# One more chunk in the seven-product form: the second layer of a fused FFT filter and two-layer network on one Trainium2 core

## The chip, the cores and the metric

The kernel runs on one core of one Trainium2 chip. The metric is the device time of one execution in microseconds (us), the median over several executions of the same program; lower is better. Engines are named as the profile names them: PE is TensorE's matmul, PEld its weight load, DVE is VectorE, ACT is ScalarE, POOL is GpSimd, SP is the queue on SyncE that issues most transfers.

## The reference, cut to what matters

```python
# x: 8 x 3008 x 256, filter: 1505 x 256 complex, w_in: 256 x 2048, w_out: 2048 x 256
X = np.fft.rfft(x, axis=1)
Y = X * (filt_r + 1j * filt_i)[None]
y = np.fft.irfft(Y, n=3008, axis=1)          # 8 x 3008 x 256
h = y.reshape(24064, 256) @ w_in             # 24064 x 2048
g = np.maximum(0.01 * h, h)
out = g @ w_out                              # 24064 x 256
```

## The kernel before, in words

**Two layers by chunks.** The 24064 tokens are cut into 47 chunks of 512 (`NCHUNK`, counted from 0). `moe1` computes the first layer of a chunk: per 128 columns of `w_in` two matmuls into one half of a wide PSUM tile `ph` (L514), and after each pair of halves one ACT activation of 1024 columns into `gt_c` (L519). The second layer of chunk `ci` is spread over the time in which `moe1` works on chunk `ci + 1`; this stretch is called the slot of chunk `ci` below.

**Two forms of the second layer.** `plain(ci)` multiplies `gt_c` by `w_out`: 4 token tiles of 16 matmuls with 256 columns (L681), each tile emptied by a DVE copy (L686) and stored. `products(ci)` treats the multiplication as a 2 x 2 block product and does it with seven half-size products instead of eight: 7 x 16 matmuls of 128 columns (L589). For this DVE builds four sums of 128 x 2048 elements beforehand (`act_sums`, L555; three go into `big[0]`, one over a quarter of `gt_c`), and every product is emptied by its own addition on DVE (L617, L625, L633, L639, L642, L653) or by an ACT copy (m1, L629). The sums of the weights, `wt_sb`, are built early, at planned times 10 to 11.5. The seventh product, `last_product`, needs the last sum and is done in the slot of the next chunk; its place in the first slot of the form is filled with sixteen items that do nothing.

`W0 = 3` says from which chunk on the second layer uses `products`; chunks 0, 1 and 2 use `plain`.

**Banks.** Tiles of the second layer alternate between two PSUM banks, `out_banks`: `psp_last` (named `pf` in the profile, the third of the `pf` tiles) and `po_ps`. `product` picks its bank when the list of work is built; `plain` picks it when the work is issued, from the final count of products:

```python
po = out_banks[(done["products"] + tj) % 2].rearrange("p a t d -> p (a t d)")[:, :D]
```

**The FFT of the next batches beside it.** Between these matmuls lie the four steps of the next batch's filtering, each with one of two more banks (`pf`): `s1_group` (L259, emptied by ACT at L262), `s2_group` (two matmuls L308, emptied by DVE with products by the filter: L314, L315 and L320 for even groups of batch 1, L317 and L320 for the others), `sa_group` (L330, emptied by ACT L332) and `sb_group` (L351, emptied into `yt` at L341). For odd groups SP moves the halves of a product across partitions (L318, L319). POOL then adds both products into `y` (L323), the moving operand of L330. POOL also issues the loads of `x` (L196). Transfers through DRAM, issued by SP, turn the data between the steps: stores L264 and L334, loads L271 and L278.

**Order.** Nothing is scheduled at run time. Every step gets a planned time (`at`, with 8 units for a slot) and the program is written in the order of these times, so each engine executes its own list in that fixed order and waits on semaphores. `plan` and the queue below it place the FFT steps. The items of the second layer are spread evenly over a slot, the sums at the offsets `SUMS`.

Of the kernel before, what the change touches and what calls it, by code (L numbers as in the profile page):

```python
# [75 lines left out]
def kernel(  # L76
# [19 lines left out]
    SL = 8  # L96
    NCH = NCT // 2
    QT = 4 * N1
    W0 = 3
    GAP = 0.6  # L100
    EXG = 0
    LANDED = 2.43
# [512 lines left out]
    def last_product(ci):  # L615
        def after(po):
            add(rows(ci, 0)[:, :, 1], po, rows(ci, 1)[:, :, 2], AL.add)  # L617
            soon(AFTER[5], lambda: stores(ci, 0))
        return product(ci, lambda: sum_places(ci)[3], b22, after, 3)

    def products(ci):
        a11, a12, a21, a22 = (lambda i=i, j=j: quarter(ci, i, j) for i in range(2) for j in range(2))

        def after5(po):
            add(rows(ci, 1)[:, :, 1:3], twice(po), part[1], AL.add)  # L625
            soon(AFTER[5], lambda: stores(ci, 1))

        def m1():
            return product(ci, a11, b11, lambda po: nc.scalar.copy(t1, po))  # L629

        def m2(early=None):
            def after(po):
                add(rows(ci, 0)[:, :, 0], po, t1, AL.add)  # L633
                if early is not None:
                    soon(0.3, lambda: [store(ci, 2 + t, rows(ci, 0)[:, t, 0], 0, P) for t in range(2)])
            return product(ci, a12, b21, after)

        def m7():
            return product(ci, lambda: sum_places(ci)[1], wt[2], lambda po: add(v7, po, t1, AL.add), 1)  # L639

        def m6(of=None):
            return product(ci, lambda: sum_places(ci)[2], wt[1], lambda po: add(part[1], twice(po), part[0], AL.add), 2, of)  # L642

        if ci == NCHUNK - 1:
            free = [w[:, :CH].rearrange("p (a t d) -> p a t d", a=2, t=2)[:, 0] for w in wide + single]
            return last_product(ci - 1) + m1() + m7() + m2(ci) + m6(free[0]) + last_three(ci, free[1:])
        if ci > W0:
            items = m1() + last_product(ci - 1) + m2() + m7()
        else:
            done["products"] += 1  # L650
            items = m1() + [lambda: None] * (2 * NCH) + m2() + m7()
        items += m6()
        items += product(ci, a22, wt[3], lambda po: add(rows(ci, 1)[:, :, 0], po, u3, AL.add))  # L653
        return items + product(ci, lambda: sum_places(ci)[0], wt[0], after5, 0)

    def last_three(ci, free):

        free += [b[:, 0] for b in out_banks]
        low, high = rows(ci, 0), rows(ci, 1)

        def m4_tile(t, po):
            add(high[:, t, 0], po, u3[:, t], AL.add)
            parts = list(pieces(ci, t, high[:, t, 0:2, :].rearrange("p k d -> p (k d)")))
            parts.sort(key=lambda v: -v[1].shape[0])
            soon(0.02, lambda: (nc.sync, nc.scalar)[t].dma_start(*parts[0]))
            for v in parts[1:]:
                soon(0.6, lambda v=v: nc.sync.dma_start(*v))

        def m3_tile(t, po):
            add(low[:, t, 1], po, high[:, t, 2], AL.add)  # L670
            soon(0.02, lambda: store(ci, 2 + t, low[:, t, 1], P, P, queue=(nc.sync, nc.scalar)[t]))

        items = product(ci, lambda: sum_places(ci)[0], wt[0], lambda po: add(high[:, :, 1:3], twice(po), part[1], AL.add), 0, free[0])
        items += product(ci, lambda: quarter(ci, 1, 1), wt[3], None, of=[f[:, 0] for f in free[1:3]], each=m4_tile)
        return items + product(ci, lambda: sum_places(ci)[3], b22, None, 3, of=[f[:, 0] for f in free[3:5]], each=m3_tile)

    def plain(ci):

        def one(tj, ct):
            po = out_banks[(done["products"] + tj) % 2].rearrange("p a t d -> p (a t d)")[:, :D]  # L680
            nc.tensor.matmul(po, gts[ci][:, ct, ts(tj, P)], w_out_sb[:, ct, :],  # L681
                             start=(ct == 0), stop=(ct == NCT - 1))
            if ct < NCT - 1:
                return
            ot = outp.tile([P, D], FP32, tag="ost", padded_shape=[P, 6 * P], name=f"ost_c{ci}_t{tj}")
            nc.vector.tensor_copy(ot[:], po)  # L686
            soon(AFTER[5], lambda: store(ci, tj, ot[:]))
        return [lambda tj=tj, ct=ct: one(tj, ct) for tj in range(4) for ct in range(NCT)]
# [70 lines left out]
    for ci in range(NCHUNK + 1):  # L759
# [3 lines left out]
        if ci == 0:  # L763
            continue
        wino = W0 <= ci - 1
        items = products(ci - 1) if wino else plain(ci - 1)
# [38 lines left out]
```

## Time and profile before

| what | value |
|---|---|
| median of 3 runs | 747.57 us (746.96 to 748.95) |
| profiled execution: its own time, first to last instruction (span) | 745.2 us |
| median less that span | 2.4 us |
| granted TensorE clock | 0.999 |
| busy, share of the span | PE 99%, PEld 71%, DVE 68%, ACT 75%, POOL 22% |
| L681, plain second layer (3 chunks) | 192 matmuls |
| slot of chunk 2, 80.37 to 97.09 us | PE 16.72, DVE 8.23, ACT 12.85, POOL 9.23 busy |
| slot of chunk 3, 97.09 to 112.02 us | PE 14.77, DVE 7.08, ACT 13.58, POOL 0.00 busy |

Only the span is listed for the profiled execution, not a total of its own; the three runs beside it are separate. The matmul rows of a timeline give the start and the modelled duration up to the result; since matmuls are pipelined, what one costs is the distance from start to start. A slot is found in the timeline by its first second-layer matmul.

### The profile page before, as it was taken

The numbers are of one execution on the slowest core, as the hardware profiler recorded it, in microseconds if no ns is written. First come the engines' busy times: TensorE is split into PE (matmuls) and PEld (weight loads), VectorE is DVE, ScalarE is ACT, GpSimd is POOL, SyncE is SP. The second block draws the span as 40 slices with busy tenths as digits, with TensorE's granted clock in tenths as the row PEclk, the third lists the DMA queues.
The fourth block names the chain that finished last, engine by engine and source line by source line (L and its number), as shares of the span: only waits on it lengthen the run. The fifth ranks groups of instructions, "written<-read, shape, count | busy, mean of one in ns | idle before, by whom it ended". The sixth has DMA issues, their size and how long they took to land.

```text
span 745.2 us, 19416 instructions
## 1 busy us (share of the span) xinstructions
PE 738.0 (99%) x8017; PEld 528.9 (71%) x8017; DVE 504.6 (68%) x686; ACT 559.1 (75%) x755; POOL 166.2 (22%) x171
## 2 busy tenths in 40 slices
PE   9999999999999999999999999999999999999997
PEld 3556667677687777877778777777777777777776
DVE  5987637766776766766777667766677676465566
ACT  4776787888878787877777787787777777777762
POOL 6503412332232212121232222121212210000000
PEclk9999999999999999999999999999999999999999
DMA  9997797888876666655675656543554333111012
GB/s 207 229 224 197 191 224 216 209 195 208 216 181 147 159 186 176 169 138 163 193 178 150 159 155 175 156 139 109 144 160 119 106 103 103 60 55 55 29 46 70
DMA packets 119848, 113.64 MB, mean 152 GB/s; under 512 B 16384, under 2 KB 93056, under 8 KB 119568
## 3 DMA queue, kind: packets, MB, share of 16 engines
q1 hardware_dynamic: 104425, 94.73, 42.9%
q0 software_dynamic: 15056, 17.49, 15.8%
q8 instruction: 62, 1.02, 0.6%
q14 instruction: 26, 0.21, 0.1%
q10 hardware_dynamic: 279, 0.19, 0.1%
HBM read 57.51 MB, written 50.33 MB: 145 GB/s over the span
## 4 chain that ended last, share of the span: by engine, by line
PE 96%; DMA 1%; DVE 1%; ACT 1%; issue 0%; ACTq 0%; DVEq 0%
PE ph L514 43%; PE pf L589 18%; PE po_ps L589 18%; PE pf L259 3%; PE pf L351 3%; PE pf L308 2%; PE pf L330 2%; PE po_ps L373 1%; PE pf L681 1%; PE po_ps L681 1%; DMA dz<-big 1%; DMA big<-dz 0%; ACT yt L341 0%; PE pf L442 0%; PE ph L401 0%
## 5 line engine op out<-in xcount | busy, mean ns | idle before, releaser
L519 ACT ACTIVATE gt_c<-ph 128x1024 f16<-128x1024 f32 x376 | 385.3, 1025 | 133.5 <-PE ph L514 122.8
L514 PE MATMUL ph<-yt,w_in_sb 128*128 128x512 f16 (+7 forms) x1728 | 447.3, 351 | 0.2 <-ACT yt L341 0.2
L589 PEld LDWEIGHTS <-gt_c 128*128 128x128 f16 x2800 | 202.2, 98 | 91.1
L323 POOL TENSOR_TENSOR y_b_g<-p_b_g,p_b_g 128x512 f16<-128x512 f32 x84 | 116.4, 1388 | 414.9 <-DMA p_b_g<-p_b_g 249.9
L589 PEld LDWEIGHTS <-big 128*128 128x128 f16 x2128 | 151.2, 98 | 61.4
L514 PEld LDWEIGHTS <-w_in_sb 128*128 128x128 f16 x1728 | 137.5, 98 | 19.7 <-DVE yt L341 0.4
L317 DVE TENSOR_TENSOR p_b_g<-pf,fb_sb 128x512 f32<-128x512 f32 x78 | 53.7, 688 | 31.0 <-PE pf L308 13.8
L589 PE MATMUL po_ps<-wt_sb,gt_c 128*128 128x128 f16 x704 | 70.0, 219 | 0.0
L589 PE MATMUL pf<-wt_sb,gt_c 128*128 128x128 f16 x688 | 68.4, 219 | 0.0
L589 PE MATMUL pf<-w_out_sb,gt_c 128*128 128x128 f16 x720 | 67.9, 219 | 0.0
L589 PE MATMUL pf<-wt_sb,big 128*128 128x128 f16 x704 | 67.2, 219 | 0.0
L262 ACT CAST big<-pf 128x512 f16<-128x512 f32 x98 | 57.1, 588 | 11.9 <-PE pf L259 10.5
L589 PE MATMUL po_ps<-w_out_sb,gt_c 128*128 128x128 f16 x688 | 66.0, 219 | 0.0
L589 PE MATMUL po_ps<-wt_sb,big 128*128 128x128 f16 x688 | 65.3, 219 | 0.0
L341 ACT CAST yt<-pf 128x376 f16<-128x376 f32 x120 | 56.4, 473 | 10.9 <-PE pf L351 8.0
L555 DVE TENSOR_TENSOR big<-gt_c 128x2048 f16<-128x2048 f16 (+1 forms) x46 | 58.7, 1276 | 0.1
L555 DVE TENSOR_TENSOR gt_c<-gt_c 128x2048 f16<-128x2048 f16 x43 | 57.4, 1335 | 1.0
L320 DVE TENSOR_TENSOR p_b_g<-pf,fa_sb 128x512 f32<-128x512 f32 x84 | 57.2, 681 | 0.2
L555 DVE TENSOR_TENSOR big<-gt_c,big 128x2048 f16<-128x2048 f16 (+1 forms) x45 | 55.3, 1230 | 0.0
L555 DVE TENSOR_TENSOR big<-big,gt_c 128x2048 f16<-128x2048 f16 (+1 forms) x45 | 55.2, 1227 | 0.1
L332 ACT CAST big<-pf 128x512 f16<-128x512 f32 x84 | 49.0, 584 | 4.9 <-PE pf L330 3.0
L259 PE MATMUL pf<-x_sb,small_sb 94*128 94x512 f16 x109 | 41.6, 381 | 0.0
(97 smaller groups left out, 625.9 us busy)
## 6 DMA issues: line engine op xcount, KB each, us to landing
dz<-big SPq DMA_DIRECT2D x98, 256.0 KB
p_b_g<-p_b_g SPq DMA_DIRECT2D x156, 128.0 KB
out_dram<-ost_c_h SPq DMA_DIRECT2D x118, 128.0 KB
big<-dz SPq DMA_DIRECT2D x42, 256.0 KB
big<-dz SPq DMA_DIRECT2D x56, 192.0 KB
x_sb<-in_x_dram POOLq DMA_DIRECT2D x40, 192.0 KB, 4.4
x_sb<-in_x_dram POOLq DMA_DIRECT2D x2, 768.0 KB, 9.1
w_in_sb<-in_moe_w_in_dram POOLq DMA_DIRECT2D x1, 1024.0 KB, 13.2
```

Of the source, the lines that this page charges most:

```text
L259: nc.tensor.matmul(ps, fwd1[:N1], x_sb[:N1, ds(2 * g, 2), :], start=True, stop=True)
L262: copy(st[:, ds(2 * (g % 2), 2), :], ps)
L317: nc.vector.tensor_tensor(p2[:], ps, fb, AL.mult)
L320: nc.vector.tensor_tensor(p1[:], ps, fa, AL.mult)
L323: ("y", b, g), lambda: nc.gpsimd.tensor_tensor(y1[:], p1[:], p3[:], AL.add)))
L332: nc.scalar.copy(st2[h % 4][:, ds(2 * (g % 2), 2), :], ps)
L341: copy(yv, ps.rearrange("p c a -> p a c"))
L351: nc.tensor.matmul(ps[:, j, :], z2[h % 4][:K4, j, ts(dt, P)], i1_sb[:K4, 4 * h + j, :], start=True, stop=True)
L514: nc.tensor.matmul(ph[:, j, ds(t - ci * CH, e - t)], w_in_sb[:, dt, ts(ct, P)], yt[:, dt, ds(t % N, e - t)], start=(dt == 0), stop=(dt == ...
L519: nc.scalar.activation(gts[ci][:, ds(2 * g, 2), :], ph, AF.Lrelu)
L555: nc.vector.tensor_tensor(*(v[:, ds(c0, n)] for v in (o, i0, i1)), op)
L589: nc.tensor.matmul(of[t], a()[:, c, ts(t, P)], w[:, c, :], start=(c == 0), stop=(c == NCH - 1))
```

## The change

The constant that says from which chunk on the seven-product form is used goes from 3 to 2, so that the second layer of chunk 2 is done by `products` and no longer by `plain`:

```diff
-    W0 = 3
+    W0 = 2
```

What follows from the one constant in the issued program: in the slot of chunk 2 (after 64 matmuls L681 are gone) there are six products, with the sixteen empty items after the first; the seventh product of chunk 2 stands in the slot of chunk 3, where the empty items were. DVE gets 4 sums L555 and 6 additions there and loses 4 copies L686; ACT gets one copy L629. Of the stores, four tiles of `ost_c` spread over the slot become two groups of three stores, the first behind L625 at the end of the slot, the second behind L617 in the next slot. The number of products rises from 305 to 312, so the tiles of `plain` in chunks 0 and 1 swap their banks: the last tile of chunk 1 now lies in `po_ps`, as does the first product of chunk 2. The FFT steps keep their order.

## The prediction

> **What bounds the kernel now.** First the page's busy time and the head of its chain, then the timeline around the slot of chunk 2, then the waits.
>
> ```profile
> PE 738.0 (99%) x8017; PEld 528.9 (71%) x8017; DVE 504.6 (68%) x686; ACT 559.1 (75%) x755; POOL 166.2 (22%) x171
> ...
> PE 96%; DMA 1%; DVE 1%; ACT 1%; issue 0%; ACTq 0%; DVEq 0%
> ```
>
> PE never rests, at a granted clock of 0.999; the list of waits on PE holds six entries of 1.2 us or less. So PE work that goes away is gained in full, and any new wait of PE is lost in full, since PE is as full after it as before.
>
> Timeline of PE (start, duration, engine, line):
>
> ```profile
> 52.02 0.60 PE L681 MATMUL pf<-w_out_sb,gt_c 128*128 128x256 f16 x4
> 52.46 0.59 PE L514 MATMUL ph<-yt,w_in_sb 128*128 128x512 f16 x2
> ...
> 85.91 0.38 PE L330 MATMUL pf<-y_b_g,small_sb 128*128 128x512 f16 x1
> ...
> 92.21 0.38 PE L330 MATMUL pf<-y_b_g,small_sb 128*128 128x512 f16 x1
> ...
> 108.04 0.55 PE L589 MATMUL po_ps<-wt_sb,gt_c 128*128 128x128 f16 x7
> 108.43 0.59 PE L514 MATMUL ph<-yt,w_in_sb 128*128 128x512 f16 x2
> ```
>
> Start to start, a plain matmul costs 0.44/4 = 0.109 us, a product matmul 0.39/7 = 0.0557 us. The two L330 are marks for later: each may only start when DVE's L320 has emptied the same bank.
>
> **The gain.** 64 x 0.109 = 6.98 us go, 112 x 0.0557 = 6.24 us come: -0.74 us on PE. In place: the slot of chunk 2 loses 6.98 and gets 96 x 0.0557 = 5.35 (-1.63), the slot of chunk 3 gets 16 x 0.0557 = 0.89 more. On POOL and SP no instruction is added but two groups of stores for four.
>
> The Trainium skill, "TensorE: Matmul & The Clock Gate", section "Back-to-back issue gap", speaks against the change: streams of weight load and matmul are to settle at about 81 ns per matmul for 128 columns. The 0.0557 above disagrees; by the page the products would cost 112 x 0.081 = 9.07 us (an estimate), and PE would lose 2.1 us instead of gaining 0.74.
>
> **The DVE list in the slot.** DVE is busy 8.23 of 16.72 us there. Added are 4 L555 of 1.22 = 4.88 and additions of 0.42 + 0.42 + 0.69 + 0.42 + 0.69 = 2.64; four copies of 0.42 go. 14.1 of some 16 us is room on average, but the list is in fixed order, and each sum stands ahead of something PE waits for. DVE before:
>
> ```profile
> 80.14 0.42 DVE L686 COPY ost_c_t<-pf 128x256 f32<-128x256 f32 x1 [1.52 <-PE pf L681]
> ...
> 84.71 0.68 DVE L320 TENSOR_TENSOR p_b_g<-pf,fa_sb 128x512 f32<-128x512 f32 x1
> ...
> 91.01 0.68 DVE L320 TENSOR_TENSOR p_b_g<-pf,fa_sb 128x512 f32<-128x512 f32 x1
> ```
>
> Step by step, with 0.06 us from an end to PE's start (a guess; 0 to 0.15):
>
> 1. Bank. The last tile of chunk 1 and the first product now share `po_ps`. The copy L686 ends at 80.56, PE is there at 80.37, and starts at 80.65 by two roundings: **+0.28** (0.2 to 0.4). Before, it took the other bank and waited for nothing.
>
> 2. The empty items. Between L330 of group 4 and L308 of group 9, which use one bank, lay five L681 and a pair L514 (0.98 us); now one L589 and two L514 (0.49 us). ACT's L332 takes 0.42 from L330's start to its own (82.43 to 82.85) and 0.58: PE arrives about 0.4 early. **+0.44** (0.2 to 0.5).
>
> 3. The sums ahead of group 9. DVE: L555 80.59 to 81.81; L314, L315, L320 (0.70 + 0.71 + 0.61) to 83.83; the second L555 to 85.05; L317 0.60; L320 85.65 to 86.34, against 85.39 before. PE's L330 of group 5 stood at 85.91; by then 23 L681 (2.51) are replaced by 25 L589 (1.39), and 0.72 was lost: 85.51. It starts at 86.40: **+0.89** (0.6 to 1.1).
>
> 4. POOL. A DVE sum and POOL's L323 do not run together. Later in the run:
>
> ```profile
> 207.33 1.22 DVE L555 TENSOR_TENSOR big<-gt_c 128x2048 f16<-128x2048 f16 x1
> 208.58 2.17 DVE L555 TENSOR_TENSOR gt_c<-gt_c 128x2048 f16<-128x2048 f16 x1
> ...
> 207.40 2.27 POOL L323 TENSOR_TENSOR y_b_g<-p_b_g,p_b_g 128x512 f16<-128x512 f32 x1 [7.20 <-DVE p_b_g L320]
> ```
>
> The first L555 takes its usual 1.22, L323 lasts a microsecond over its 1.27, the next L555 a microsecond over its 1.22: they take turns. In this slot L323 now meets sums. `y` of group 8 becomes ready at 83.9 behind the second L555, runs 85.05 to 86.3; the third L555 then runs to 87.5; `y` of group 7 holds to 88.8. DVE's L314 of group 10 overwrites what that L323 reads, so it starts at 88.8 (87.62 before). Then 2.02, the fourth L555 1.22, L639 0.42: 92.5. The fifth product's bank waits for this L639, PE being there at 92.26: **+0.29** (0 to 0.6). L317 0.60 and L320 to 93.8. PE's L330 of group 7 stood at 92.21; 47 L681 (5.12) against 67 L589 (3.73) and 1.90 lost: 92.72. It waits to 93.8: **+1.10** (0.5 for no meeting with POOL, 1.4 if POOL takes two turns).
>
> The waits sum to 3.0 us.
>
> 5. Transfers. Before, PE lost 0.16 at 109.24 to the load L278 of turned data (issued 106.21, landing 2.98 later), behind the last store L334 (issued 100.69, 5.51 to land). Behind the three stores of chunk 2, held by L625 to about 99.2 and issued at 0.82 each (98.18, two in 1.65), L334 comes 1.5 later; the second group of stores puts 256 KB, 0.9 us at the 280 GB/s of that stretch, ahead of L278: 2.4 later in all. PE is 2.26 later there. So the 0.16 stays, between 0 and 0.5 if the queues drain otherwise. The `x` loads on POOL move 2.1 (92.51 to 94.6) behind L323; the next L259 that needs one stood at 100.36, and moves too; landing takes 3.6 to 7.7 us. Nothing is lost in the middle case, up to 1 in the late one.
>
> 6. The rest. ACT gets one L629 of 0.39 beside 12.85 of 16.72 busy: nothing, since its L519 waited 0.17 to 0.8 on PE here; without that cover it is 0.27 once. Swapped banks later on are the same two banks in turn: nothing. In the slot of chunk 3, L617 and a sum that starts about 1.4 us late sit on a DVE busy 7.08 of 14.93 us: nothing, and 0.4 if a bank is missed.
>
> Sum: -0.74 + 3.0 = **+2.3 us**. The profiled span goes from 745.2 to 747.5; what lies around it, 2.4 us to the median, stays: 747.57 + 2.3 = **749.9 us**.
>
> **The rivals.**
>
> *Covers hold.* The waits do not form, since DVE has 2 us of room on average and PE often runs one bank ahead: -0.74 us, 746.8. For it speaks that PE hardly waited beside the some 170 sums of later slots; against it that the list of groups 8 to 11 has no later slot's spacing and that L330 trails L320 by only 0.5 us before (85.39 to 85.91). It decides if L320 of group 9 ends before 85.5.
>
> *No meeting with POOL.* Steps 1 to 3 with 0.65 in step 4: +1.5 us, 749.1. It holds if L323 lies beside PSUM work only; the fixed order speaks against.
>
> *Late transfers.* Delayed L323 and L625 push `x` loads and L278 past PE, each once by 0.5 to 1.5: +3.3 to +5 us, 750.9 to 752.6. For it: 5.51 us for one store and 2.98 for one load on the way to PE already; against: PE comes 2.3 us later as well.
>
> *Weight loads pace the products.* If loads didn't overlap, 112 x 0.098 (mean of a weight load) = 10.98 us, +4.0 in place of -0.74, and with the waits +7. The x7 row says no. The page of the Trainium skill named above, "TensorE: Matmul & The Clock Gate", gives a milder form of this rival.
>
> **How the numbers follow.** Forecast 0.50, late transfers 0.27, no meeting 0.12, covers hold 0.08, weight loads 0.03. A measurement of this kernel tells about 0.3%, 2.24 us, from no change; the forecast lies on that bound, 0.27 of its 0.50 above. Slower by over 0.3%: 0.27 + 0.27 + 0.03 = 0.57. Within: 0.23 + 0.12 + 0.05 = 0.40. Faster: 0.03, covers that hold and a scatter of the runs as wide as before's 2 us. The range leaves out most of the covers case and the top of the late one: 747.5 to 751.8. Its low end is the sum of the low ends of the waits, 1.5, less 0.74, and another 0.8 for scatter; its high end is that of the high ends, 4.0 less 0.74, and the 1 of late transfers.
>
> **What would show it.** PE waits named to DVE of about 0.3, 0.9, 0.3 and 1.1 and one to ACT of 0.4, all between 80 and 94; PE's busy sum 0.74 lower; L323 of group 8 at 85, lasting over 2 us with its wait; slot of chunk 2 near 18.1 us long (16.72 - 1.63 + 3.0) and of chunk 3 near 15.8 (14.93 + 0.89). If PE waits for a DMA by over 0.5 us after 98, the late case is it; no wait over 0.2 in the slot makes the forecast wrong.

## The result, and the profile after

The changed kernel takes 750.75 us (median of 8 runs, 748.41 to 752.74), the kernel before beside it 747.88 (8 runs, 746.54 to 749.28). The ratio is 1.004, interval 1.0031 to 1.005: slower by 2.9 us, 2.3 to 3.7. The forecast was 749.9, slower by 2.3.

A part of every time lies outside the span. The forecast put it at 2.4 us, the difference between a median and the span of another execution, and let it stay. Run by run it is 2.1 to 2.3 us in the 57 executions of the kernel before that stand beside the experiments, and 1.8 to 1.9 in the eight of the changed kernel. So the span grew by some 0.3 us more than the time did; no run explains this difference.

The profiled execution has a span of 750.4 us against 745.2 and took 752.28 in all, 1.5 above the median of its kernel. The 5.2 us between the two spans are therefore not the effect of the change alone, and what follows goes by single places. First line 1 of the page:

```profile
PE 739.0 (98%) x8065; PEld 529.1 (71%) x8065; DVE 509.3 (68%) x692; ACT 560.1 (75%) x756; POOL 168.4 (22%) x171
```

The matmuls are 48 more (112 for 64), and PE has 1.0 us more busy time, where 0.74 less was forecast. Busy time runs to the modelled end of the last matmul ahead of each wait, and there are more waits now; the starts below are the better measure. The list of waits on PE (sum, times, longest, in us) has new entries, and the one for L278 stood at 0.2 before:

```profile
PE pf L330 <- DVE p_b_g L320: 1.5, 2, 0.9
PE pf L351 <- DMA big<-dz: 1.5, 1, 1.5
...
PE pf L330 <- POOL y_b_g L323: 0.6, 1, 0.6
...
PE pf L308 <- ACT big L332: 0.2, 1, 0.2
```

The entry for POOL is a wait at 542.17, taken up under "Left open"; the timeline of PE shows where the others are (the bracket is idle time after the modelled end of the matmul before; from start to start the loss is about 0.17 larger):

```profile
80.28 0.59 PE L514 MATMUL ph<-yt,w_in_sb 128*128 128x512 f16 x2
80.96 0.55 PE L589 MATMUL po_ps<-w_out_sb,gt_c 128*128 128x128 f16 x7
...
83.15 0.59 PE L514 MATMUL ph<-yt,w_in_sb 128*128 128x512 f16 x2
83.93 0.38 PE L308 MATMUL pf<-big,f_sb 128*128 128x256 f16 x2 [0.19 <-ACT big L332]
...
85.40 0.50 PE L589 MATMUL pf<-w_out_sb,gt_c 128*128 128x128 f16 x6
86.57 0.38 PE L330 MATMUL pf<-y_b_g,small_sb 128*128 128x512 f16 x1 [0.67 <-DVE p_b_g L320]
...
92.25 0.33 PE L589 MATMUL pf<-wt_sb,big 128*128 128x128 f16 x3
92.75 0.33 PE L589 MATMUL po_ps<-wt_sb,gt_c 128*128 128x128 f16 x3 [0.17 <-DVE big L639]
93.94 0.38 PE L330 MATMUL pf<-y_b_g,small_sb 128*128 128x512 f16 x1 [0.87 <-DVE p_b_g L320]
...
98.58 0.39 PE L589 MATMUL po_ps<-w_out_sb,gt_c 128*128 128x128 f16 x4
...
100.78 0.44 PE L589 MATMUL pf<-w_out_sb,big 128*128 128x128 f16 x5
101.36 0.38 PE L330 MATMUL pf<-y_b_g,small_sb 128*128 128x512 f16 x1
...
111.55 0.22 PE L589 MATMUL pf<-wt_sb,gt_c 128*128 128x128 f16 x1
113.27 0.35 PE L351 MATMUL pf<-i_sb,big 96*128 96x94 f16 x4 [1.50 <-DMA big<-dz]
```

The rows of the kernel before on which the last line of the table below and the shift rest:

```profile
79.94 0.59 PE L514 MATMUL ph<-yt,w_in_sb 128*128 128x512 f16 x2
...
108.86 0.22 PE L589 MATMUL po_ps<-wt_sb,gt_c 128*128 128x128 f16 x1
109.24 0.35 PE L351 MATMUL pf<-i_sb,big 96*128 96x94 f16 x4 [0.16 <-DMA big<-dz]
```

Each loss is the start of the waiting matmul less the start of the row above it and that row's matmuls at 0.0557 (L589) or 0.2165 (L514) each. The first product: 80.96 - 80.28 - 2 x 0.2165 = 0.25. By the same rule L351 lost 0.32 before and 1.66 after.

| place | forecast | measured |
|---|---|---|
| bank of the first product, 80.96 | 0.28 | 0.25 |
| L308 behind ACT's L332, 83.93 | 0.44 | 0.35 |
| L330 of group 5 behind L320 of group 9, 86.57 | 0.89 | 0.84 |
| bank of the fifth product, 92.75 | 0.29 | 0.33 |
| L330 of group 7, 93.94 | 1.10 | 1.02 |
| L330 of group 11 behind POOL, 101.36 | 0 | 0.30 |
| L351 behind L278, 113.27 | 0 (to 0.5) | 1.34 more than before |

The first five sum to 2.79 (3.0 forecast). The slot of chunk 2 goes from 80.71, when the L514 of 80.28 are through, to 98.58: 17.87 us, 18.1 forecast. The slot of chunk 3 goes on to 116.06: 17.48 us, where 15.8 was forecast. With the gain of 0.74 and the last two rows the net is 3.69; from the starts of L351, 113.27 - 109.24 = 4.03, less the 0.34 by which this slot began later (L514 at 80.28 against 79.94), it is the same. DVE and POOL beside it:

```profile
80.48 0.42 DVE L686 COPY ost_c_t<-po_ps 128x256 f32<-128x256 f32 x1 [1.52 <-PE po_ps L681]
...
84.10 1.22 DVE L555 TENSOR_TENSOR gt_c<-gt_c 128x2048 f16<-128x2048 f16 x1
...
85.83 0.68 DVE L320 TENSOR_TENSOR p_b_g<-pf,fa_sb 128x512 f32<-128x512 f32 x1
86.43 2.32 DVE L555 TENSOR_TENSOR big<-big,gt_c 128x2048 f16<-128x2048 f16 x1
...
92.28 0.41 DVE L639 TENSOR_TENSOR big<-po_ps,big 128x256 f32<-128x256 f32 x1
...
93.21 0.68 DVE L320 TENSOR_TENSOR p_b_g<-pf,fa_sb 128x512 f32<-128x512 f32 x1
```

```profile
84.33 3.33 POOL L323 TENSOR_TENSOR y_b_g<-p_b_g,p_b_g 128x512 f16<-128x512 f32 x2 [4.24 <-PE pf L308]
...
91.38 3.34 POOL L323 TENSOR_TENSOR y_b_g<-p_b_g,p_b_g 128x512 f16<-128x512 f32 x2 [3.23 <-DVE p_b_g L320]
...
99.29 2.02 POOL L323 TENSOR_TENSOR y_b_g<-p_b_g,p_b_g 128x512 f16<-128x512 f32 x1 [3.58 <-PE pf L259]
101.26 1.53 POOL L196 DMA_DIRECT2D x_sb<-in_x_dram  x3
```

DVE has no idle time from the copy L686 to the end of L642; before, it had idle time in this stretch. Where a sum meets L323, one of the two is 0.8 to 1.1 us longer: the third L555 takes 2.32 for 1.22, two L323 take 3.33 for the 2.50 that they take without sums.

### The profile page after: what moved, and what is told of

Its sections match the earlier page's. It is cut to its first block, busy times and chain, and to the rows that moved or that the text cites. A ratio compares the mean times of both kernels' runs of the same rounds, so it can differ in the third digit from the quotient of the medians.

```text
span 750.4 us, 19518 instructions
## 1 busy us (share of the span) xinstructions
PE 739.0 (98%) x8065; PEld 529.1 (71%) x8065; DVE 509.3 (68%) x692; ACT 560.1 (75%) x756; POOL 168.4 (22%) x171
## 4 chain that ended last, share of the span: by engine, by line
PE 80%; DMA 5%; POOL 1%; SPq 1%; issue 0%; DVE 0%; ACT 0%; POOLq 0%; DVEq 0%
PE ph L514 37%; PE po_ps L589 17%; PE pf L589 17%; DMA p_b_g<-p_b_g 3%; PE pf L351 2%; PE pf L259 2%; PE pf L330 2%; PE pf L308 2%; POOL y_b_g L323 1%; DMA dz<-big 1%; DMA big<-dz 0%; SPq L318 0%; PE ph L589 0%; SPq L575 0%; SPq L271 0%
## 5 line engine op out<-in xcount | busy, mean ns | idle before, releaser
L514 PE MATMUL ph<-yt,w_in_sb 128*128 128x512 f16 (+7 forms) x1728 | 447.5, 351 | 0.2 <-ACT yt L341 0.2
L589 PEld LDWEIGHTS <-gt_c 128*128 128x128 f16 x2864 | 206.8, 98 | 95.9 <-issue 2.8
L323 POOL TENSOR_TENSOR y_b_g<-p_b_g,p_b_g 128x512 f16<-128x512 f32 x84 | 118.6, 1414 | 418.9 <-DMA p_b_g<-p_b_g 249.5
L589 PEld LDWEIGHTS <-big 128*128 128x128 f16 x2176 | 154.9, 98 | 63.2
L514 PEld LDWEIGHTS <-w_in_sb 128*128 128x128 f16 x1728 | 136.9, 98 | 20.1 <-issue 1.1
L317 DVE TENSOR_TENSOR p_b_g<-pf,fb_sb 128x512 f32<-128x512 f32 x78 | 53.6, 687 | 30.4 <-PE pf L308 15.3
L589 PE MATMUL po_ps<-w_out_sb,gt_c 128*128 128x128 f16 x752 | 71.2, 219 | 0.1
L589 PE MATMUL pf<-wt_sb,gt_c 128*128 128x128 f16 x720 | 71.0, 219 | 0.0
L589 PE MATMUL po_ps<-wt_sb,gt_c 128*128 128x128 f16 x704 | 70.6, 219 | 0.2 <-DVE big L639 0.2
L589 PE MATMUL pf<-wt_sb,big 128*128 128x128 f16 x720 | 68.7, 219 | 0.0
L589 PE MATMUL po_ps<-wt_sb,big 128*128 128x128 f16 x704 | 67.2, 219 | 0.0
L589 PE MATMUL pf<-w_out_sb,gt_c 128*128 128x128 f16 x688 | 65.8, 219 | 0.0
L555 DVE TENSOR_TENSOR big<-gt_c 128x2048 f16<-128x2048 f16 (+1 forms) x47 | 59.3, 1262 | 0.1
L555 DVE TENSOR_TENSOR gt_c<-gt_c 128x2048 f16<-128x2048 f16 x44 | 58.0, 1319 | 1.0
L320 DVE TENSOR_TENSOR p_b_g<-pf,fa_sb 128x512 f32<-128x512 f32 x84 | 57.1, 680 | 0.2
L555 DVE TENSOR_TENSOR big<-big,gt_c 128x2048 f16<-128x2048 f16 (+1 forms) x46 | 56.9, 1238 | 0.1
L555 DVE TENSOR_TENSOR big<-gt_c,big 128x2048 f16<-128x2048 f16 (+1 forms) x46 | 55.8, 1214 | 0.0
L332 ACT CAST big<-pf 128x512 f16<-128x512 f32 x84 | 49.0, 584 | 6.7 <-PE pf L330 4.8
```

The source lines that it names most:

```text
L317: nc.vector.tensor_tensor(p2[:], ps, fb, AL.mult)
L320: nc.vector.tensor_tensor(p1[:], ps, fa, AL.mult)
L323: ("y", b, g), lambda: nc.gpsimd.tensor_tensor(y1[:], p1[:], p3[:], AL.add)))
L332: nc.scalar.copy(st2[h % 4][:, ds(2 * (g % 2), 2), :], ps)
L514: nc.tensor.matmul(ph[:, j, ds(t - ci * CH, e - t)], w_in_sb[:, dt, ts(ct, P)], yt[:, dt, ds(t % N, e - t)], start=(dt == 0), stop=(dt == ...
L555: nc.vector.tensor_tensor(*(v[:, ds(c0, n)] for v in (o, i0, i1)), op)
```

## The experiments

Every ratio is to the kernel before on the same chip. In the traces the *shift* is by how much later than before ACT's L629 of chunk 4 starts, less the shift that was there already when the slot of chunk 2 began; it is 3.69 for the changed kernel. "Landing" is the time from the issue of the store L334 that holds back L278 to the issue of L278. A trace is one execution. Those of e1 and e7 lie 1.5 and 2.3 us above the median of their runs, those of e6 and e4 0.9 and 2.1 below; those of the other experiments lie within 0.8. Where the work is the same, the waits in the slot of chunk 2 repeat from trace to trace; a wait for a transfer in one of these four need not be that of a median run.

### e2: without the sums

The forecast's theory puts nearly all of the loss on the four sums of chunk 2, since all that PE waits for stands behind them.

```diff
-        nc.vector.tensor_tensor(*(v[:, ds(c0, n)] for v in (o, i0, i1)), op)
+        if ci != 2:
+            nc.vector.tensor_tensor(*(v[:, ds(c0, n)] for v in (o, i0, i1)), op)
```

> W0 = 2, the four sums of chunk 2 on DVE left out (its products read what lies there). Theory: PE's waits on L320 (0.84 and 1.02 us) and on the bank of L639 (0.33) go, the waits on the bank (0.25) and on ACT (0.35) stay, so PE comes out of the slot 2.2 us earlier than in the changed kernel. L625 and L617 then come earlier too, but the load L278 waits for its own store: PE may wait there 0.5 to 2 us. Over the kernel before: 0 to +1.5 us. Rival (transfers alone make the loss): the time stays within 0.5 us of the changed kernel, +2.4 to +2.9.

Measured: 747.57, ratio 1.0002 (0.9993 to 1.0011); shift -0.47. Of the new waits of PE, one stays:

```profile
PE pf L308 <- ACT big L332: 0.2, 1, 0.2
```

The bank of the first product still costs its 0.25 by the starts (80.81 - 80.13 - 2 x 0.2165), too short for the list. L351 no longer waits (landing 5.90). With the 0.32 that L351 lost before, -0.74 + 0.25 + 0.35 - 0.32 = -0.46 is the shift. The products, the empty items, the additions and the regrouped stores are all still there and cost little; the loss needs the sums, the wait for L278 included.

### e5: the sums alone

The other way round: chunk 2 stays `plain`, and DVE gets the four sums at their places, into buffers that nobody reads then.

```diff
+    def spare_sum(step):
...
+        for step, time in enumerate(SUMS if ci == W0 else ()):
+            at(SL * ci + time, lambda step=step: spare_sum(step))
```

> W0 = 3 as before; only four sums of the operands of chunk 2 are added on DVE at the times at which the changed kernel has them, into buffers that nobody reads, and chunk 2 stays plain. PE's work is that of the kernel before. Theory (the sums on DVE, not the products, cost the time): L320 of groups 9 and 11 end near 86.4 and 93 to 94 as in the changed kernel, the third sum meets L323 and takes over 2 us, PE waits 0.3 to 0.6 on the first and 1.0 to 1.5 on the second, and again on L278: +1.5 to +3 us over the kernel before. Rival (the order of PE's new items, the empty items and the banks make the loss): within 0.5 us of the kernel before.

Measured: 751.43, ratio 1.0055 (1.0042 to 1.0068), more than expected; shift +3.7. Its waits of PE, and the fourth sum, which here meets L323 (the third does too, with 2.00):

```profile
94.55 0.38 PE L330 MATMUL pf<-y_b_g,small_sb 128*128 128x512 f16 x1 [1.63 <-DVE p_b_g L320]
...
113.16 0.35 PE L351 MATMUL pf<-i_sb,big 96*128 96x94 f16 x4 [1.74 <-DMA big<-dz]
```

```profile
91.05 2.25 DVE L563 TENSOR_TENSOR big<-gt_c,big 128x2048 f16<-128x2048 f16 x1
```

Neither product nor bank nor store was changed, and the time is lost at three of the same places: by the starts 0.31 at L330 of group 5 (too short for a bracket), 1.79 at L330 of group 7 and 1.58 more than before at L351, 3.68 together and so all of the shift. The expectation named all three, gave no size for the wait for L278, and had too little for that on group 7 (1.0 to 1.5). With e2: the sums in DVE's list cause the loss, and are enough for it.

### e1: the bank of the first product

```diff
-            po = out_banks[(done["products"] + tj) % 2]...
+            po = out_banks[(done["products"] + tj + 1) % 2]...
```

> W0 = 2, but the plain tiles of chunks 0 and 1 get the banks that they had with W0 = 3, so the last tile of chunk 1 and the first product of chunk 2 no longer share po_ps. Theory (each DVE or ACT wait in the slot of chunk 2 is paid by PE in full): the wait of 0.25 us before the first product is gone, but the waits behind it on L320 do not shrink by much, since DVE's list sets them; 0 to 0.25 us under the changed kernel, so about +2.6 to +2.9 us over the kernel before. Rival (one lost bank turn shifts everything that follows): 1 us or more is won back.

Measured: 751.16, ratio 1.0042 (1.0028 to 1.0056); shift +3.68. The first product starts without a wait, and the next wait for DVE is longer:

```profile
87.53 0.38 PE L330 MATMUL pf<-y_b_g,small_sb 128*128 128x512 f16 x1 [0.92 <-DVE p_b_g L320]
```

0.92 for 0.67: the 0.25 of the bank came back in full. Step 1 of the forecast is a wait that forms, but not a cost that adds: DVE's list sets when L320 of group 9 ends, and PE spends the time before it in one wait or another.

### e4: a small addition on POOL

For groups 7 to 10 of batch 1 POOL adds only 16 of the 256 columns, after setting the tile to zero.

```diff
-                ("y", b, g), lambda: nc.gpsimd.tensor_tensor(y1[:], p1[:], p3[:], AL.add)))
...
+                soon(y_delay(b, g), lambda: nc.gpsimd.memset(y1[:], 0.0))
...
+                *(v[:, :, : 16 if few else D] for v in (y1, p1, p3)), AL.add)))
```

> W0 = 2, POOL's L323 for groups 7 to 10 of batch 1 adds only 2 x 16 of 2 x 256 columns and fills the rest with zeros first. Theory (a sum and a full L323 take turns): the third sum takes 1.22 us and not 2.32, L314 of group 10 starts near 88 and not 89.12, PE's wait on L639's bank goes and that on L320 of group 11 falls from 1.02 to 0.65 or less; the wait on L320 of group 9 (0.84) stays. 0.7 to 1.0 us under the changed kernel, +1.9 to +2.2 over the kernel before. Rival (DVE's own list is long enough to hold PE up): all waits of PE stay within 0.1 us.

Measured: 750.07, ratio 1.0028 (1.0018 to 1.0038): 0.9 us by the ratios less than the change, as expected, though the intervals overlap. The trace is clearer:

```profile
85.73 1.22 DVE L558 TENSOR_TENSOR big<-big,gt_c 128x2048 f16<-128x2048 f16 x1
```

```profile
85.87 0.38 PE L333 MATMUL pf<-y_b_g,small_sb 128*128 128x512 f16 x1 [0.67 <-DVE p_b_g L320]
...
92.44 0.38 PE L333 MATMUL pf<-y_b_g,small_sb 128*128 128x512 f16 x1 [0.39 <-DVE p_b_g L320]
```

The third sum has its 1.22 back, the bank of the fifth product no wait, and group 7 loses 0.39 instead of 0.87; group 9, whose L320 stands behind sums that kept their 1.22 in both kernels, stays at 0.67. This is step 4 of the forecast, taken away alone. The wait for L278 is 0.30 in this trace; since this execution lies 2.1 us below its median, how much of that is the edit is not shown.

### e3: later stores

To tell the loss at L278 apart: the two groups of output stores of chunk 2 go behind it.

```diff
-            soon(AFTER[5], lambda: stores(ci, 0))
+            soon(2.5 if ci == 2 else AFTER[5], lambda: stores(ci, 0))
-            soon(AFTER[5], lambda: stores(ci, 1))
+            soon(4.8 if ci == 2 else AFTER[5], lambda: stores(ci, 1))
```

> W0 = 2, the two groups of three output stores of chunk 2 issued behind the loads L278 of batch 1. Theory: PE's wait for L278 (1.50 us at 113 in the changed kernel, 0.16 before) goes back to 0 to 0.4, all waits in the slot of chunk 2 stay; 1.0 to 1.4 us under the changed kernel, +1.5 to +1.9 over the kernel before. Rival (the transfer waits because POOL's and DVE's steps came late, not because of the stores): L351 still waits 1 us or more and the time does not move.

Measured: 750.74, ratio 1.0043 (1.0031 to 1.0056): no gain, against the expectation. L351 does not wait (landing 6.36), but the moved stores now stand ahead of the loads L271, and PE waits there:

```profile
120.79 0.38 PE L308 MATMUL pf<-big,f_sb 128*128 128x256 f16 x2 [1.20 <-DMA big<-dz]
```

### e8: the stores alone

Chunk 2 stays `plain`, and its four stores are put off into two late groups.

```diff
-            soon(AFTER[5], lambda: store(ci, tj, ot[:]))
+            soon(max(AFTER[5], (32.4 if tj < 2 else 34.6) - clock["now"]) if ci == 2 else AFTER[5], ...)
```

> W0 = 3, all work as before; only the output stores of chunk 2 are issued in two groups at the places that they have in the changed kernel, behind the end of the slot. Theory (the wait on L278 comes of DVE's and POOL's late steps with the stores ahead of it): PE waits on L278 0.2 to 0.8, no other wait: 0 to +0.7 us. Rival (the stores alone make the 1.5 us): PE waits 1.2 us or more on L278, +1 us or more.

Measured: 747.76, ratio 1.0004 (0.9995 to 1.0013). PE waits 0.93 for L278, between what the theory (0.2 to 0.8) and the rival (1.2 or more) had; the shift is 0.78. The landing is a short 5.35; it is the issue of L334 that is late, at 101.46 for 100.69. The time is at most 1.0 longer. Late stores alone are a part of that wait and not all of the loss.

### e9: the loads of `x` earlier

In the traces the landing was long where the last three loads L196 were issued a short time ahead of the store. Here the loads go ahead of the L323 that holds them up.

```diff
-                at(s1 + xl + x_step * g, ...
+                at(29.9 if 29.9 < s1 + xl + x_step * g < 40 else s1 + xl + x_step * g, ...
```

> W0 = 2, only the three loads of x that stand on POOL behind L323 of group 11 (issued from 101.3 in the changed kernel, 1.3 before the last store L334) are put ahead of that L323, so that they go out near 96 to 97.5. All waits in the slot of chunk 2 stay. Theory (these loads crowd the last store L334, which took 7.4 us to land against 5.5 before, and L278 and PE's L351 wait for it): L334 to L278 takes 5.5 to 6.2 us, PE's wait for L278 falls from 1.5 to 0.5 or less; 0.8 to 1.3 us under the changed kernel, +1.5 to +2.1 over the kernel before. Rival (the store is slow because of the output stores around it): L334 to L278 stays over 7 us and the time does not move.

Measured: 750.53, ratio 1.0033 (1.0021 to 1.0045). SP of the changed kernel, then of e9:

```profile
99.72 2.30 SPq L575 DMA_DIRECT2D out_dram<-ost_c_h  x3
...
102.61 0.45 SPq L334 DMA_DIRECT2D dz<-big  x1
...
110.02 1.94 SPq L278 DMA_DIRECT2D big<-dz  x4
```

```profile
99.35 3.39 SPq L575 DMA_DIRECT2D out_dram<-ost_c_h  x3
...
103.54 1.16 SPq L334 DMA_DIRECT2D dz<-big  x1
...
108.99 1.75 SPq L278 DMA_DIRECT2D big<-dz  x4
```

The landing falls from 7.41 to 5.45, that of the kernel before (5.52). But the three output stores ahead now take 3.39 to issue, L334 goes out 0.9 later by the clocks of the traces (1.3 from the start of the slot), and L351 still waits 1.23. The crowd moved from the landing to the issue, and most of the delay with it; neither theory's expectation came in whole. Over all traces:

| | before | e2 | e6 | e8 | e9 | e4 | e5 | e3 | e7 | e1 | after |
|---|---|---|---|---|---|---|---|---|---|---|---|
| row of the last three loads L196 to issue of L334 | 5.2 | 4.6 | 4.3 | 5.6 | about 8 | 2.5 | 2.8 | 1.1 | 1.3 | 1.3 | 1.4 |
| landing | 5.5 | 5.9 | 6.0 | 5.4 | 5.5 | 6.6 | 7.1 | 6.4 | 7.3 | 7.6 | 7.4 |

Loads over 4 us ahead: 5.4 to 6.0. Loads under 3 us ahead: 6.4 to 7.6, the least of them in e3, which has no output stores there. The loads come late because POOL executes them behind L323 of group 11, which the sums put off (94.24 before, 99.29 after).

### e7 and e6: the sums elsewhere

Both put the sums of chunk 2 at other places, the first two in parts ahead of the slot; e7 does this alone, e6 also undoes the shared bank and puts the empty items behind the second product.

```diff
+    FIRST_SUMS = ((-0.45, 0, 0, 6), (-0.35, 1, 0, 4), (0.05, 0, 6, 2), (0.6, 1, 4, 4), (2.35, 2), (5.75, 3))
...
-            for time, *what in [(v, i) for i, v in enumerate(SUMS)] if ci < NCHUNK else LAST:
+            for time, *what in FIRST_SUMS if ci - 1 == W0 else [(v, i) for i, v in enumerate(SUMS)] if ci < NCHUNK else LAST:
```

And in e6 alone, with the bank as in e1:

```diff
-            items = m1() + [lambda: None] * (2 * NCH) + m2() + m7()
+            items = m1() + m2() + [lambda: None] * (2 * NCH) + m7()
```

> W0 = 2, only the sums of chunk 2 cut up and moved as in the repaired kernel; the empty items and the banks stay as in the changed kernel. Theory: the waits on L320 go, those of 0.25 (bank) and 0.35 (ACT) stay: -0.4 to +0.4 us against the kernel before. Rival (bank and empty items set off the later waits): +1 us or more.

> W0 = 2 with the same work as the changed kernel in another order: the sums of chunk 2 cut up and set where DVE is idle (first sum 6 of 8 columns and half of the second ahead of the slot, the rest behind L320 of groups 8, 9 and 11), the sixteen empty items behind the second product instead of the first, and the old banks for chunks 0 and 1. Theory: all waits of PE in the slot fall under 0.2 us, that on L278 under 0.4; the gain of 0.74 shows: -0.8 to 0 us against the kernel before. Rival (the form itself costs PE something that is not seen in its waits): +0.5 us or more with no waits in the slot.

Measured: e7 748.41, ratio 1.0016 (1.0008 to 1.0025), more than its expectation; e6 747.83, ratio 1.0007 (0.9999 to 1.0016), where -0.8 to 0 us was expected. In e7 the waits for L320 are gone, but a part of a sum now stands ahead of the copy that frees the shared bank, and the wait for L278 is there again at 1.55:

```profile
81.75 0.55 PE L591 MATMUL po_ps<-w_out_sb,gt_c 128*128 128x128 f16 x7 [0.67 <-DVE ost_c_t L688]
```

In e6 the wait for the bank and the wait for L278 are both gone. No wait of PE in the slot is long enough for a bracket; by the starts 0.26 and 0.28 are left, at L330 of groups 5 and 7:

```profile
84.22 0.60 PE L514 MATMUL ph<-yt,w_in_sb 128*128 128x512 f16 x2
84.91 0.38 PE L330 MATMUL pf<-y_b_g,small_sb 128*128 128x512 f16 x1
...
90.38 0.33 PE L591 MATMUL po_ps<-wt_sb,gt_c 128*128 128x128 f16 x3
90.83 0.38 PE L330 MATMUL pf<-y_b_g,small_sb 128*128 128x512 f16 x1
```

With the 0.32 that L351 lost before, -0.74 + 0.26 + 0.28 - 0.32 = -0.52 is the shift. So most of the loss belongs to the order of DVE's list and not to the products themselves: with another order the third chunk can take the form at no loss that the times can tell. But the 0.74 that PE saves did not appear in the time either; e6 is no faster than the kernel before, and its median span is 0.7 longer (746.0 for 745.3). The trace shows how: against the kernel before, PE later loses 0.51 around 215.95, where a product waits for its bank (the entry below in the list of waits), and 0.40 at 536.87 behind POOL. What sets these later waits is not shown.

```profile
PE po_ps L591 <- DVE big L641: 0.4, 1, 0.4
```

## Why the prediction was right, and where it was off

**The bound and the gain.** That a new wait of PE is lost in full held. Six L589 from 96.78 to 97.11 are 0.055 each, as in the row of before; the rule of the Trainium skill ("TensorE: Matmul & The Clock Gate", "Back-to-back issue gap") that puts such matmuls at 81 ns, and with it the rival of weight loads, had no part: e2 has all 112 of them and is not slower. The gain of 0.74 is needed to make up the shift of e2; in the times it lies below what they can tell.

**Steps 1 to 4** were each within 0.1 us of their wait, the sum at 2.79 for 3.0. What they got wrong is that step 1 adds: e1 showed that the wait behind it absorbs it. A sum of waits at the places where they form gives the right end, since each step was worked out with the loss before it, but a single term of it is not what its removal would bring.

**Step 4**, the turn-taking with POOL, came with its size, but in another order: the forecast let the third sum run first and the second L323 hold up L314; in the trace L323 went first and the sum took 2.32. The end is the same: L320, for which L330 of group 7 waits, ended at 93.89, which is 93.55 without the slot's own 0.34, against 93.8. The rival without a meeting falls by e4. The Trainium skill, "SBUF — State Buffer", section "Who interferes with whom", says that a DVE instruction with two inputs in SBUF contends with a GpSimd instruction that reads SBUF; the trace agrees (2.32 for 1.22). L317 and L320, which read one input from PSUM, keep 0.68.

**Step 5 was mis-sized.** It put 0 to 0.5 on L278, and the trace has 1.34 more than before. Without the slot's own 0.34, the store L334 was issued 1.58 later (forecast 1.5), and PE reached L351 2.35 later (forecast 2.26). The term that failed is the 0.9 for the second group of output stores: the landing grew by 1.89, from 5.52 to 7.41, and L278 went out 3.47 later where 2.4 was forecast. That leaves 3.47 - 2.35 = 1.12, and the load itself took 0.2 longer. The rows of before:

```profile
100.69 0.36 SPq L334 DMA_DIRECT2D dz<-big  x1
...
106.21 1.74 SPq L278 DMA_DIRECT2D big<-dz  x4
```

```profile
94.24 1.27 POOL L323 TENSOR_TENSOR y_b_g<-p_b_g,p_b_g 128x512 f16<-128x512 f32 x1 [0.69 <-PE ph L514]
95.45 1.52 POOL L196 DMA_DIRECT2D x_sb<-in_x_dram  x3
```

The step let the `x` loads move by 2.1 and priced only who needs `x`, not what they do to a store that follows them. The last three moved by 5.8 (101.26 against 95.45), because L323 of group 11, behind which they stand, moved by 5.1. Of these, 2.9 are the later exchange L319 that this L323 needs (its issue ends at 95.17 for 92.27); the other 2.2 pass between that and the start of L323 (4.1 for 2.0), for which the forecast had no term either. In e4, e7 and e9 this stretch is 3.5 to 4.0, and the profile names the transfer itself as what L323 waited for. This same L323 cost L330 of group 11 its 0.30, for which the forecast had no term.

**The rivals.** Covers that hold would have needed L320 of group 9 to end before 85.5; it ended at 86.51, or 86.17 without the 0.34. The late transfers came in on top of the forecast, not instead of it. By the forecast's own sign for that rival, a wait for a DMA of over 0.5 us after 98, the traced execution is the late case: L351 waits 1.50. In the trace the sum is 3.7, inside the rival's 3.3 to 5; in the times it is 2.9 (2.3 to 3.7), between the two cases. The rival starts from the late L323 and L625, and what makes these late is the sums: without them L351 does not wait (e2).

**What was luck.** Steps 1 to 4 with the gain give 2.79 - 0.74 = 2.05 of the 2.9. What fills the rest has no term of its size in the sum: the waits at L330 of group 11 and at L278 (1.64 in the trace) and later ones add to it, and the 0.3 us outside the span takes from it. That the median shows only 0.9 of them is luck for the number.

**Left open.** How much of the 1.34 a run without the profile's surplus of 1.5 us has is not known; e3 and e9 moved that wait without gaining it. Behind chunk 4 the profiled execution loses 1.13 more, 0.73 of it at one place:

```profile
542.17 0.38 PE L330 MATMUL pf<-y_b_g,small_sb 128*128 128x512 f16 x1 [0.56 <-POOL y_b_g L323]
```

It is there in e1, e6 and e7 too, at 0.4 to 0.7, and at 0.19 in e9, but not in e2, e3, e4, e5 or e8, though e3 has the same order of work there as the changed kernel. No run explains it.

## What to carry to other kernels

Work taken off the engine that bounds the kernel is paid for where the substitute work queues: here 0.74 us less on PE put four sums, 4.9 us, in fixed order ahead of the instructions that free PE's banks, on an engine that was half idle on average. Cost such a change by going through the other engine's list in order and comparing the end of each bank-freeing instruction with the start of the matmul that wants the bank; the share of busy time says nothing of it. Then follow what the delay pushes, down to the DMA issues behind it, and look at which other transfers they now meet.

## What was not expected of the hardware

A store on its way (L334, issue to the release of L278) took 5.4 to 6.0 us where loads issued by POOL were over 4 us ahead of it, and 6.4 to 7.6 where they were less than 3 us ahead. Issuing them earlier brought the landing back to 5.45, but three output stores on SP then took 3.39 us to issue instead of 2.30.

A short addition on POOL is not spared: of 16 of the 256 columns in e4, it took 1.10 us where the sum of 83.40 to 84.62 was under way, and 0.25 where none was:

```profile
83.63 1.10 POOL L325 TENSOR_TENSOR y_b_g<-p_b_g,p_b_g 128x32 f16<-128x32 f32 x1 [3.40 <-DVE p_b_g L320]
...
85.27 0.25 POOL L325 TENSOR_TENSOR y_b_g<-p_b_g,p_b_g 128x32 f16<-128x32 f32 x1
```
